# A hand-fixed instruction order written anew for a gated linear-attention and erf-feed-forward kernel

## The chip, the cores and the metric

The kernel runs on one core of a Trainium2 chip. The metric is device time in microseconds of one execution; lower is better. Three timed executions of the kernel before took 673.87, 674.10 and 674.49 us, a median of 674.1 us.

## What is computed

The reference takes `q`, `k`, `v` and complex gates `a_re`, `a_im` of shape (4 batches, 8 heads, 768 steps, 48 channels), and float64 weights `w_in` (384 x 2048) and `w_out` (2048 x 384). Cut to what matters:

```python
mag = np.sqrt(a_re * a_re + a_im * a_im)
scale = np.minimum(mag, 0.999) / (mag + 1e-06)
a_re_n, a_im_n = (a_re * scale, a_im * scale)
for t in range(S):                       # complex state of 48 x 48 per head
    S_re, S_im = ar * S_re - ai * S_im + kv[t], ar * S_im + ai * S_re
    y[t] = q[t] @ S_re
x = y.transpose(0, 2, 1, 3).reshape(3072, 384)
h = x @ w_in
sp = np.maximum(h, 0.0) + np.log1p(np.exp(-np.abs(h)))   # softplus
out = (h * erf(sp)) @ w_out
```

## The kernel before

The 3072 tokens are cut into 12 units of 256 tokens, three to a batch, and each unit into two chunks of 128 (`C = 2`). The order writes them as `u.c`, so `7.1` is the second chunk of unit 7.

**Gates.** `g` loads the gates, `m` squares them, `t` and `o` form the ratio of the two parts, `l` takes logarithms of the magnitude, `r` the arctangent. `a` turns the angles into running sums over time by a matmul with an upper triangle (`sum`, lines 914 and 915 or 995 and 997) and `F`, the rounded-off turn (line 1002); `s` takes sine and cosine (`CS`). `p` does the same for the decay: a running sum (line 1018, or 914 and 915) and its exponentials with both signs (`pr`). From unit 2 on a running sum is split into a high and a low fp32r part; the low part is made on VectorE (lines 961 and 987).

**Attention of one chunk.** `k`, `q` and `v` load; `K` and `Q` multiply by `pr` and `CS` (lines 1042 and 1047) and, from unit 2 on, transpose blocks on VectorE into `X`, which `M` moves by twelve small DMAs into `KQ` (line 1064). In units 0 and 1, `kT` and `qT` do this on TensorE. `A` forms the masked scores of four heads (matmuls at line 1084, mask on VectorE at line 1088). `S` carries the state (lines 1103, 1109, 1112). `Y` forms the result (line 1139), which ScalarE copies to `xT` (line 1141).

**Feed-forward of one unit.** It goes in two slabs of 1024 hidden channels, written `u.slab.i`. `h` is a tile of 256 channels: six matmuls into `hps` (line 1152) and a copy by ScalarE (line 1155). `x` is four ScalarE passes over a slab for the softplus and its inverse (exponential and logarithm). `e` is one quarter of a slab: a Gelu on ScalarE, then four VectorE operations (lines 1180 to 1186). `O` are the output products. Units 0 to 2 do them plainly (line 1220); from unit 3 on seven products of half the size (Strassen's way, line 1244) replace eight, with sums of `h` in `f` (lines 1197 and 1199) and of the products on VectorE (line 1252). The results are written to HBM from SP's queue (line 1211).

**Weights and checks.** `n` loads a piece of the float64 weights and narrows it on VectorE; `i` loads it again and looks for weights out of range (line 859); `b` forms sums of weights. `Z` checks at the end that all ranges seen allow this path: it reduces what was seen (lines 1310 to 1313), sums it over partitions with one matmul (line 1316), and compares (lines 1320 and 1321). Every engine then reads the flag `ok` and branches (lines 1388 and 1389); the slower path behind the branch is not taken here. `u4_2` and the like are four warm-up matmuls whose output nobody reads (line 1302).

**What sets the order.** Each of these steps is a Python generator, and each `yield` in it ends one part, most often the work of one engine. A string `ORDER` of 2303 names says which step goes on by one part next, and the instructions are issued in that order on every engine:

```python
with tc.manual_schedule():
    for nm in ORDER.split():
        if nm[0] == "u":
            steps[nm] = warm(int(nm[1:].split("_")[0]))
        next(steps[nm])
```

So the string fixes the list of each engine and of SP's DMA queue, and the order in which tiles take their turns in buffers. `ps_h` has two PSUM buffers for `hps`: a new `h` tile waits for the copy of the one before the last. The string was written outside the kernel by a planner that gives each part a place from assumed durations of operations, waits and transfers.

ScalarE's functions live in three sets of tables: logarithm and exponential, arctangent and sine, and Gelu. `act` issues a table load (line 786) when a function is not in the set that was loaded last, so the order of ScalarE's work decides how many loads there are:

```python
sets = [nm for nm, fs in TABLES.items() if func in fs]
if sets and T.get("table") != sets[0]:
    T["table"] = sets[0]
    scalar.preload_act_table_set(sets[0])
```

Of the kernel before, what the change touches and what calls it, by code (L numbers as in the profile page):

```python
# [49 lines left out]
u4_38 u4_21 u4_20 g0.0 g0.0 u2_39 g0.1 g0.1 t0.0 u2_34 u2_25 u4_2 m0.0 m0.0 m0.0 t0.0 t0.0 l0.0 l0.0 l0.0 l0.0  # L50
u2_40 o0.0 l0.0 m0.1 m0.1 m0.1 u2_23 p0.0 n0 n0 k0.0 t0.1 t0.1 t0.1 n0 n0 o0.1 n1 n1 l0.1 p0.0 l0.1 p0.0 l0.1
l0.1 r0.0 a0.0 l0.1 K0.0 r0.1 a0.1 q0.0 u2_24 Q0.0 u8_0 u8_1 a0.0 a0.0 u2_22 a0.0 s0.0 s0.0 s0.0 u2_41 a0.1 p0.1
p0.1 a0.1 n1 n1 g1.0 t1.0 g1.0 n3 p0.0 g1.1 Q0.0 qT0.0.1 qT0.0.0 qT0.0.0 K0.0 kT0.0.0 n3 a0.1 kT0.0.1 t1.0 p0.1
qT0.0.1 kT0.0.0 A0.0.0 t1.0 n3 o1.0 kT0.0.1 n3 v0.0 S0.0 r1.0 s0.1 a1.0 s0.1 a1.0 g1.1 A0.0.0 k0.1 p0.0 p0.1
q0.1 K0.1 Q0.1 S0.0 s0.1 K0.1 m1.1 m1.1 m1.0 a1.0 m1.0 Q0.1 m1.0 l1.0 l1.0 v0.1 A0.0.1 A0.0.1 n2 a1.0 n2 q1.0
t1.1 kT0.1.1 S0.1 l1.0 kT0.1.1 S0.1 l1.0 n2 l1.0 qT0.1.1 qT0.1.1 Y0.0 m1.1 n2 t1.1 t1.1 p0.1 S0.1 qT0.1.0
qT0.1.0 kT0.1.0 kT0.1.0 l1.1 Y0.0 l1.1 p1.0 p1.0 p1.0 l1.1 A0.1.0 A0.1.0 A0.1.1 A0.1.1 o1.1 r1.1 s1.0 l1.1 a1.1
s1.0 s1.0 n4 n4 Q1.0 k1.0 n4 l1.1 n4 Y0.1 Y0.1 a1.1 n5 n5 Q1.0 n5 K1.0 n5 p1.1 p1.1 g2.1 g2.0 t2 g2.1 g2.0 n6
v1.0 m2 m2 m2 v1.1 q1.1 t2 n6 K1.0 n7 h0.0.6 h0.0.6 v2.0 t2 l2 p1.1 l2 a1.1 l2 l2 p1.0 p1.1 a1.1 n6 Q1.1 n6 o2
n7 n7 l2 qT1.0.0 qT1.0.0 s1.1 n8 k1.1 l2 l2 a2.0 q2.0 h0.0.4 h0.0.4 s1.1 s1.1 qT1.0.1 h0.0.0 qT1.0.1 n7 Q1.1 n8  # L60
kT1.0.1 kT1.0.1 h0.0.2 r2 kT1.0.0 kT1.0.0 h0.0.2 h0.0.0 x0.0 a2.0 a2.0 S1.0 K1.1 S1.0 A1.0.1 p2.0 p2.0 p2.0
A1.0.0 h0.1.6 h0.1.6 a2.0 a2.0 a2.0 n8 A1.0.1 n9 x0.0 e0.0.2 p1.0 a2.0 n8 a2.1 A1.0.0 K1.1 a2.1 n9 a2.1 e0.0.0
S1.0 h0.1.0 h0.1.0 Y1.0 Y1.0 qT1.1.0 qT1.1.0 qT1.1.1 a2.1 n9 Q2.0 n9 qT1.1.1 a2.1 a2.1 a2.1 kT1.1.1 kT1.1.1 n10
n10 n10 p1.1 kT1.1.0 kT1.1.0 s2 s2 s2 p2.1 p2.1 p2.1 A1.1.1 A1.1.1 n10 k2.0 K2.0 A1.1.0 A1.1.0 S1.1 Q2.0 K2.0
S1.1 q2.1 K2.0 Q2.0 g3.0 g3.1 t3 t3 m3 g3.1 g3.0 t3 Q2.1 o3 m3 r3 h0.1.4 h0.1.4 Y1.1 Y1.1 h0.1.2 S2.0 a3.0
h0.1.2 m3 l3 l3 l3 h1.0.0 p2.0 n11 n11 Q2.1 n11 a3.0 S1.1 n11 S2.0 h1.1.0 x0.0 a3.0 a3.0 k2.1 K2.1 l3 l3 l3 l3
a3.0 M2.0 M2.0 M2.0 M2.0 A2.0.0 A2.0.1 K2.1 A2.0.1 A2.0.0 p2.0 p3.1 h1.0.0 x0.0 p3.0 a3.1 a3.1 e0.0.2 h1.0.2
h1.1.0 a3.1 p3.1 p3.1 a3.1 a3.1 e0.0.0 e0.0.2 e0.0.0 p3.0 p3.0 h1.0.2 e0.0.2 a3.1 e0.0.2 e0.0.0 a3.1 e0.0.0
e0.0.6 h1.0.4 h1.0.4 s3 K2.1 n12 k3.0 g4.0 e0.0.4 g4.0 g4.1 p3.0 q3.0 g4.1 Y2.0 n13 s3 s3 Q2.1 e0.0.4 e0.0.6
S2.0 e0.0.4 e0.0.4 e0.0.4 m4 m4 m4 l4 l4 t4 t4 l4 e0.0.6 e0.0.6 e0.0.6 h1.0.6 h1.1.6 M2.1 M2.1 M2.1 M2.1 l4 K3.0  # L70
n12 n12 l4 Q3.0 Q3.0 l4 K3.0 l4 Q3.0 h1.0.6 q3.1 p3.1 O0.0 v3.0 p3.0 O0.1 O0.3 O0.5 O0.7 A2.1.1 t4 A2.1.0 O0.2
A2.1.1 o4 O0.4 O0.6 h1.1.4 A2.1.0 k3.1 x0.1 x0.1 n12 x0.1 x0.1 K3.0 e0.1.2 e0.1.2 e0.1.2 e0.1.2 e0.1.0 e0.1.0
e0.1.2 h1.1.4 h1.1.6 Y2.0 r4 e0.1.0 e0.1.0 e0.1.0 v3.1 a4.0 a4.0 v2.1 Y2.1 e0.1.6 Y2.1 e0.1.6 e0.1.4 e0.1.6
e0.1.4 e0.1.4 e0.1.4 a4.0 a4.0 n13 e0.1.6 n13 h1.1.2 S3.0 S3.0 n13 h1.1.2 x1.0 x1.0 O0.9 h2.0.0 a4.0 a4.0 a4.0
e0.1.6 n15 e0.1.4 n15 n15 x1.0 M3.0 x1.0 h2.0.6 M3.0 M3.0 M3.0 A3.0.0 v4.1 n14 e1.0.0 K3.1 n15 a4.1 Q3.1 a4.1
e1.0.0 h2.0.0 e1.0.0 e1.0.0 e1.0.2 e1.0.2 n14 a4.1 a4.1 e1.0.2 p4.1 O0.8 e1.0.0 e1.0.2 e1.0.2 p4.1 p4.1 A3.0.1
h2.0.6 p4.0 O0.10 O0.11 p4.0 p4.0 h2.0.2 h2.0.2 g5.1 k4.0 n14 n14 k4.1 e1.0.4 e1.0.6 e1.0.6 g5.0 m5 t5 a4.1 g5.0
g5.1 e1.0.6 m5 K3.1 e1.0.4 e1.0.4 m5 e1.0.4 e1.0.4 A3.0.0 K3.1 p3.1 q4.1 Q3.1 A3.0.1 e1.0.6 e1.0.6 Q3.1 M3.1
M3.1 h2.1.0 h2.1.2 O0.12 h2.1.0 x1.1 t5 O0.14 a4.1 l5 O0.14 x1.1 l5 a4.1 h2.0.4 O0.13 S3.1 O0.15 O1.1 O1.3 O1.5
h2.1.2 O1.7 l5 l5 l5 S3.1 l5 K4.0 l5 x1.1 O0.15 x1.1 s4 S3.1 t5 o5 e1.1.2 e1.1.2 e1.1.2 e1.1.0 e1.1.0 e1.1.0  # L80
e1.1.2 e1.1.2 e1.1.0 e1.1.0 O1.0 h2.1.6 O1.2 O1.4 Y3.0 s4 r5 s4 K4.0 e1.1.4 e1.1.4 e1.1.4 e1.1.6 e1.1.6 e1.1.6
a5.0 q4.0 M3.1 p4.0 M3.1 A3.1.1 O1.6 A3.1.0 a5.0 A3.1.1 A3.1.0 e1.1.6 Q4.0 e1.1.4 K4.0 Q4.0 Q4.0 Q4.1 Q4.1 K4.1
h2.0.4 h2.1.6 h2.1.4 Y3.0 x2.0 Y3.1 v4.0 S4.0 a5.0 x2.0 a5.0 Y3.1 e1.1.4 S4.0 e1.1.6 p4.1 p4.1 M4.0 M4.0 x2.0
x2.0 M4.0 M4.0 O0.14 h3.0.0 e2.0.0 e2.0.0 e2.0.0 e2.0.2 e2.0.0 e2.0.2 e2.0.2 e2.0.2 e2.0.0 e2.0.2 p5.0 O1.9 p5.1
p5.0 p5.0 h3.0.0 h2.1.4 O1.11 O1.8 O1.10 e2.0.6 e2.0.4 a5.0 a5.0 e2.0.6 e2.0.4 a5.0 e2.0.4 e2.0.6 a5.1 a5.1 p5.1
# [24 lines left out]
h5.1.6 l8 O4.4 O4.4 O4.5 O4.5 O4.5 O4.5 e5.0.6 e5.0.4 h5.1.0 h5.1.0 O4.7 O4.7 O4.7 e5.0.4 e5.0.4 s7 s7 e5.0.6  # L110
# [1310 lines left out]
```

## Time and profile before

| what | value |
|---|---|
| median of the runs shown | 674.1 us |
| the profiled execution's own time | 674.05 us |
| its span, first to last instruction | 672.3 us |
| TensorE matmul rows, weight-load rows | 646.0 us (96%), 562.2 us (84%) |
| VectorE | 609.6 us (91%) |
| ScalarE | 578.7 us (86%), of it 120.6 us in 94 table loads |
| granted TensorE clock, mean | 0.998 |

The profile is of one execution; the sums of the prediction are made against its span. A row of the groups or of a timeline names the line, the engine, the operation, and output and inputs by the program's names; a bracket or the part after the last bar tells how long the engine was idle before and what ended that. A row of the waits reads: engine, what and line that waited, what it waited for, microseconds in total, times, and the longest. In the table by stages each engine has its busy microseconds and, in brackets, its number of instructions. A fp32 matmul appears as two passes in the rows, with a weight load for each. PE is TensorE, PEld its weight loads, DVE VectorE, ACT ScalarE, SP the engine that issues DMAs.

### The profile page before, as it was taken

The numbers are of one execution on the slowest core, as the hardware profiler recorded it, in microseconds if no ns is written. First come the engines' busy times: TensorE is split into PE (matmuls) and PEld (weight loads), VectorE is DVE, ScalarE is ACT, GpSimd is POOL, SyncE is SP. The second block draws the span as 40 slices with busy tenths as digits, with TensorE's granted clock in tenths as the row PEclk, the third lists the DMA queues.
The fourth block names the chain that finished last, engine by engine and source line by source line (L and its number), as shares of the span: only waits on it lengthen the run. The fifth ranks groups of instructions, "written<-read, shape, count | busy, mean of one in ns | idle before, by whom it ended". The sixth has DMA issues, their size and how long they took to land.

```text
span 672.3 us, 12307 instructions
## 1 busy us (share of the span) xinstructions
PE 646.0 (96%) x4728; PEld 562.2 (84%) x4728; DVE 609.6 (91%) x992; ACT 578.7 (86%) x762; POOL 1.1 (0%) x8
## 2 busy tenths in 40 slices
PE   8799999999999999999999999999999999999995
PEld 8678886876777768899898898999998899988885
DVE  5999999999989999999999999999999997868782
ACT  7999999999999999988997997998995895678800
POOL 0000000000000000000000000000000000000000
PEclk9999999999999999999999999999999999999999
DMA  9695767552256237227537736716726327211000
GB/s 252 159 247 153 169 138 143 118 129 48 36 114 123 43 61 187 54 44 169 93 51 165 130 60 149 134 26 158 137 44 168 57 34 207 39 34 47 1 24 29
DMA packets 282796, 70.23 MB, mean 104 GB/s; under 512 B 269396, under 2 KB 272488, under 8 KB 282728
## 3 DMA queue, kind: packets, MB, share of 16 engines
q1 hardware_dynamic: 280648, 68.96, 48.2%
q8 instruction: 39, 0.64, 0.4%
q10 hardware_dynamic: 2080, 0.39, 0.3%
q14 instruction: 29, 0.24, 0.1%
HBM read 48.82 MB, written 4.75 MB: 80 GB/s over the span
## 4 chain that ended last, share of the span: by engine, by line
ACT 41%; PE 24%; DVE 23%; issue 4%; DMA 4%; SPq 2%; POOL 0%; DVEq 0%; ACTq 0%; POOLq 0%
PE hps L1152 10%; ACT L786 10%; ACT z L787 7%; ACT yy L787 6%; ACT e L787 3%; DVE yy L1182 3%; DVE z L1180 3%; PE Y L1244 3%; DVE e L1184 2%; ACT h L1155 2%; ACT CS L787 2%; DVE h L1186 2%; PE X L1244 2%; ACT y L787 2%; ACT pr L787 2%
## 5 line engine op out<-in xcount | busy, mean ns | idle before, releaser
L1152 PE MATMUL hps<-xT,w_in_sb 128*128 128x256 f32 x1152 | 263.3, 381 | 1.8 <-ACT h L1155 1.2
L1152 PEld LDWEIGHTS hps<-xT,w_in_sb 128*128 128x128 f32 x1152 | 215.2, 190 | 34.7 <-ACT h L1155 5.1
L786 ACT ACT_TABLE_LOAD x94 | 120.6, 1283 | 3.7 <-issue 2.1
L1180 DVE TENSOR_TENSOR z<-z,yy 128x512 f32<-128x512 f32 x96 | 65.1, 686 | 17.7 <-ACT e L787 17.3
L787 ACT ACTIVATE e<-z 128x512 f32<-128x512 f32 x96 | 57.8, 627 | 24.7 <-DVE h L1186 23.9
L1155 ACT COPY h<-hps 128x512 f32<-128x512 f32 x96 | 54.2, 578 | 17.0 <-PE hps L1152 17.0
L1182 DVE SCALAR_TENSOR_TENSOR yy<-z,yy 128x512 f32<-128x512 f32 x96 | 65.1, 689 | 1.9
L1220 PE MATMUL ops<-w_out_sb,h 128*128 128x384 f32 x192 | 66.1, 487 | 0.0
L1186 DVE SCALAR_TENSOR_TENSOR h<-e,h 128x512 f32<-128x512 f32 x96 | 64.5, 686 | 1.4
L1184 DVE TENSOR_TENSOR e<-e,yy 128x512 f32<-128x512 f32 x96 | 64.6, 686 | 1.1
L1084 PEld LDWEIGHTS sc<-KQ 96*128 96x128 f32 x384 | 47.0, 191 | 8.2 <-issue 5.2
L1220 PEld LDWEIGHTS ops<-w_out_sb,h 128*128 128x128 f32 x192 | 35.6, 190 | 20.2 <-DVE h L1186 0.6
L1084 PE MATMUL sc<-KQ 96*128 96x128 f32 x384 | 49.9, 278 | 2.4 <-DMA KQ<-X 1.1
L787 ACT ACTIVATE z<-h 128x2048 f32<-128x2048 f32 x24 | 45.8, 1910 | 4.9 <-DVE seen L859 3.2
L787 ACT ACTIVATE yy<-z 128x2048 f32<-128x2048 f32 x24 | 45.8, 1909 | 0.7 <-DVE seen L859 0.2
L787 ACT ACTIVATE yy<-yy 128x2048 f32<-128x2048 f32 x24 | 45.9, 1911 | 0.6
L787 ACT ACTIVATE z<-z 128x2048 f32<-128x2048 f32 x24 | 45.8, 1909 | 0.4
L1139 PE MATMUL y<-A,v 128*32 128x128 f32 x768 | 34.1, 276 | 2.0 <-DVE A L1088 1.5
L1088 DVE TENSOR_TENSOR A<-sc,triu 128x512 f32<-128x512 f32 x48 | 32.0, 677 | 1.1 <-PE sc L1084 1.1
L1103 PEld LDWEIGHTS kv<-v,kt 128*96 128x96 f32 x320 | 29.8, 165 | 1.8 <-issue 0.7
L1103 PE MATMUL kv<-v,kt 128*96 128x48 f32 x320 | 29.8, 246 | 0.0
L1139 PEld LDWEIGHTS y<-A,v 128*32 128x32 f32 x768 | 21.1, 109 | 9.4 <-DVE A L1088 2.6
(114 smaller groups left out, 1070.5 us busy)
## 6 DMA issues: line engine op xcount, KB each, us to landing
KQ<-X SPq DMA_DIRECT2D x240, 64.0 KB
raw<-in_moe_w_in_dram SPq DMA_DIRECT2D x8, 768.0 KB
raw<-in_moe_w_out_dram SPq DMA_DIRECT2D x8, 768.0 KB
again<-in_moe_w_in_dram SPq DMA_DIRECT2D x8, 768.0 KB
ar<-in_a_re_dram SPq DMA_DIRECT2D x24, 192.0 KB
k<-in_k_dram SPq DMA_DIRECT2D x24, 192.0 KB
q<-in_q_dram SPq DMA_DIRECT2D x24, 192.0 KB
v<-in_v_dram SPq DMA_DIRECT2D x48, 96.0 KB
```

What stands on the lines that cost most here:

```text
L786: scalar.preload_act_table_set(sets[0])
L787: scalar.activation(func=func, **kw)
L1084: nc.tensor.matmul(out=ps[:, j, :], lhsT=head("k", g * HG + j, u, c), rhs=head("q", g * HG + j, u, c), start=True, stop=True)
L1103: nc.tensor.matmul(out=kv[0:D2, j, :], lhsT=T["kt", u, c][:, j].rearrange("p u d -> p (u d)"), rhs=side(T["v", u][:, c, j // 2], j % 2), s ...
L1139: nc.tensor.matmul(out=ps[b * QUAD:(b + 1) * QUAD, i, :], lhsT=lhsT, rhs=rhs, start=start, stop=stop)
L1152: nc.tensor.matmul(out=ps[:, e, :], lhsT=w_in_sb[:, (sl * SLAB + i) // 2, kd, e * P:(e + 1) * P], rhs=T["xT", u][:, kd, :], start=(kd == 0 ...
L1155: scalar.copy(out=T["h", u, sl][:, i:i + 2, :], in_=ps)
L1180: vector.tensor_tensor(out=z, in0=z, in1=y, op=OP.mult)
L1182: vector.scalar_tensor_tensor(out=y, in0=z, scalar=-2.0, in1=y, op0=OP.add, op1=OP.mult)
L1184: vector.tensor_tensor(out=e, in0=e, in1=y, op=OP.mult)
L1186: vector.scalar_tensor_tensor(out=h, in0=e, scalar=1.0 / RT2, in1=h, op0=OP.add, op1=OP.mult)
L1220: nc.tensor.matmul(out=ps, lhsT=lhsT, rhs=w_out_sb[:, i, :], start=i == HALF, stop=i == KF - 1)
```

## The change

Only the string `ORDER` is replaced. It holds the same 2303 names, each as often as before: no instruction is added or taken away by the string itself, but ScalarE's table loads follow from its order. The planner was run anew with somewhat longer operations, waits and transfers than the medians it had used, and was allowed to place the split running sums beside the result matmuls. Nearly every place moves. The beginning and the end of the diff:

```diff
@@ -47,125 +47,125 @@
 ORDER = """
-u4_38 u4_21 u4_20 g0.0 g0.0 u2_39 g0.1 g0.1 t0.0 u2_34 u2_25 u4_2 m0.0 m0.0 m0.0 t0.0 t0.0 l0.0 l0.0 l0.0 l0.0
-u2_40 o0.0 l0.0 m0.1 m0.1 m0.1 u2_23 p0.0 n0 n0 k0.0 t0.1 t0.1 t0.1 n0 n0 o0.1 n1 n1 l0.1 p0.0 l0.1 p0.0 l0.1
-l0.1 r0.0 a0.0 l0.1 K0.0 r0.1 a0.1 q0.0 u2_24 Q0.0 u8_0 u8_1 a0.0 a0.0 u2_22 a0.0 s0.0 s0.0 s0.0 u2_41 a0.1 p0.1
-p0.1 a0.1 n1 n1 g1.0 t1.0 g1.0 n3 p0.0 g1.1 Q0.0 qT0.0.1 qT0.0.0 qT0.0.0 K0.0 kT0.0.0 n3 a0.1 kT0.0.1 t1.0 p0.1
...
-e10.1.2 f10.1 f10.1 h11.0.2 x11.0 x11.0 x11.0 x11.0 e11.0.4 e11.0.4 e11.0.4 h11.1.6 e11.0.0 e11.0.0 e11.0.4
-e11.0.0 e11.0.4 e11.0.0 e11.0.0 h11.1.2 h11.1.2 e11.0.2 e11.0.2 e11.0.6 e11.0.2 e11.0.6 e11.0.6 e11.0.2 e11.0.2
-e11.0.6 O10.1 h11.1.0 O10.1 h11.1.0 h11.1.4 h11.1.4 x11.1 x11.1 x11.1 x11.1 e11.1.2 O10.2 O10.2 e11.0.6 O10.0
-O10.3 O10.4 O10.6 O10.5 e11.1.0 O10.5 O10.7 O10.5 O10.5 O10.7 O10.7 O10.8 O10.9 O10.4 O10.10 e11.1.2 e11.1.0
-e11.1.2 e11.1.0 e11.1.2 e11.1.0 O10.11 e11.1.2 e11.1.0 f11.0 O10.11 O10.11 O10.12 O10.13 e11.1.4 e11.1.4 e11.1.6
-e11.1.6 e11.1.4 O10.13 e11.1.6 e11.1.4 e11.1.6 e11.1.4 e11.1.6 f11.1 f11.1 O11.0 O10.13 O11.1 O11.3 O11.1 O11.2
-O11.2 f11.0 O11.4 O11.5 O11.5 O11.4 O11.6 O11.5 O11.5 O11.7 O11.7 O11.12 O11.7 O11.8 O11.9 O11.10 O11.11 O11.13
-O11.11 O11.11 Z Z O11.13 O11.13 Z
+u4_2 u4_38 u4_21 u8_0 u2_39 u4_20 g0.0 g0.0 g0.1 g0.1 u2_34 u2_41 t0.0 t0.0 m0.0 m0.0 m0.0 m0.1 l0.0 l0.0 m0.1
+l0.0 t0.1 u2_22 t0.0 o0.0 m0.1 l0.1 t0.1 l0.1 l0.1 l0.0 l0.0 p0.0 p0.0 p0.0 u8_1 n0 u2_40 r0.0 a0.0 k0.0 t0.1 n1
+l0.1 n0 l0.1 o0.1 n0 a0.0 q0.0 n0 u2_24 n1 n1 a0.0 r0.1 a0.0 Q0.0 s0.0 K0.0 g1.0 n1 u2_23 p0.1 a0.1 a0.1 u2_25
+n3 n3 v0.0 q0.1 s0.0 s0.0 Q0.0 qT0.0.0 K0.0 kT0.0.1 kT0.0.0 p0.0 p0.1 t1.0 Q0.1 n3 m1.0 p0.1 a0.1 t1.0 qT0.0.0
...
+O9.11 i15 O9.13 h11.1.6 e10.1.4 e10.1.2 e10.1.2 f10.1 f10.0 O9.11 O9.13 f10.0 f10.1 O9.13 O9.11 h11.0.2 x11.0
+x11.0 x11.0 x11.0 e11.0.4 e11.0.4 e11.0.4 O10.0 h11.1.6 e11.0.0 e11.0.0 e11.0.4 e11.0.0 e11.0.4 e11.0.0 e11.0.0
+h11.1.2 h11.1.2 e11.0.2 e11.0.2 e11.0.6 e11.0.2 e11.0.6 e11.0.6 e11.0.6 e11.0.6 i15 e11.0.2 e11.0.2 i15 h11.1.4
+h11.1.4 h11.1.0 h11.1.0 x11.1 x11.1 x11.1 x11.1 e11.1.2 O10.1 O10.3 O10.2 e11.1.0 O10.6 O10.1 O10.4 O10.2 O10.5
+O10.4 O10.5 O10.5 O10.5 O10.7 O10.7 Z O10.7 O10.8 O10.9 e11.1.2 e11.1.0 e11.1.2 e11.1.0 e11.1.2 e11.1.0 O10.10
+O10.11 e11.1.2 e11.1.0 e11.1.4 f11.0 e11.1.4 O10.12 O10.13 O10.11 e11.1.6 O10.11 O10.13 e11.1.6 e11.1.4 e11.1.6
+e11.1.4 e11.1.6 e11.1.4 O10.13 e11.1.6 f11.1 f11.1 O11.0 O11.3 O11.1 Z O11.2 O11.1 f11.0 O11.2 Z O11.4 O11.5
+O11.5 O11.5 O11.5 O11.6 O11.7 O11.7 O11.7 O11.4 O11.8 O11.9 O11.10 O11.11 O11.11 O11.11 O11.12 O11.13 O11.13
+O11.13
 """
```

Between the second slab of unit 3 and the first of unit 4 (from `x3.1` to `x4.0`) both orders do the exponentials of unit 6's decay (`p6`). The order before has `p6.0 p6.0 p6.0 O2.15 e3.1.6 e3.1.6 e3.1.4 ... p6.1 p6.1 p6.1`, with the Gelu of two quarters between the chunks; the new one has `e3.1.6 p6.1 p6.0 p6.1 ... p6.1 p6.0 p6.1 p6.1 ... p6.0 p6.0 p6.0`, with no Gelu between the exponentials.

## The prediction

> **What bounds the kernel now.** I read the busy table by stages first: three engines are above 86% over the whole span, so the page's averages settle nothing.
>
> ```profile
> core 0: us, PE busy (x) PEld busy (x) DVE busy (x) ACT busy (x) POOL busy (x), PEclk, DMA share, GB/s
> 0.00:20.00 20.00, 17.41 (x106) 15.47 (x106) 12.18 (x32) 14.97 (x30) 1.08 (x8) 1.00 0.98 236
> ...
> 100.00:200.00 100.00, 98.16 (x584) 73.42 (x583) 94.33 (x143) 98.73 (x123) 0.00 (x0) 1.00 0.50 97
> 200.00:300.00 100.00, 98.01 (x698) 79.50 (x698) 96.27 (x155) 98.11 (x122) 0.00 (x0) 1.00 0.44 86
> ...
> 400.00:500.00 100.00, 99.36 (x766) 92.22 (x765) 96.42 (x155) 90.29 (x116) 0.00 (x0) 1.00 0.54 110
> 500.00:600.00 100.00, 98.95 (x785) 90.99 (x784) 86.70 (x138) 75.37 (x90) 0.00 (x0) 1.00 0.43 93
> ```
>
> TensorE's own row says 98% everywhere; its weight loads (PEld) tell more: 73 and 80 us per 100 up to 300 us while ScalarE is at 98 to 99, then 91 to 92 while ScalarE falls to 90 and 75. So ScalarE (and close behind it VectorE) paces the first 300 us and TensorE the rest. A microsecond of ScalarE counts before 300 us and hardly after.
>
> Next, how much TensorE loses. I charge each instruction the median time from its start to the next start on its engine where nothing was waited for (an hps matmul of two passes 0.432 us, a 192-column output product 0.325 us, and so on). TensorE's whole list comes to 629.6 us, VectorE's to 591.7, ScalarE's to 559.7. What the clock is ahead of such a sum is that engine's lag. TensorE's lag is 11.2 us at 40 us, 15.0 at 100, 22.5 at 300, 30.8 at 620, and 35.1 at 660; after its last product (664.75 us) 7.5 us of closing remain. 629.6 + 35.1 + 7.5 = 672.2, the span. Nothing in the change touches the 629.6, so all it can do lies in those 42.6 us.
>
> Third, the wait views: what the lag is made of late on, and what waits are there to be won.
>
> ```profile
> ACT e L787 <- DVE h L1186: 23.9, 15, 3.9
> DVE z L1180 <- ACT e L787: 17.3, 16, 5.6
> ACT h L1155 <- PE hps L1152: 17.0, 13, 2.8
> DVE out L1252 <- PE Z L1244: 7.0, 2, 5.6
> ```
>
> The large ones are ScalarE and VectorE waiting, mostly after 300 us, where they have time to spare: 17.0 of the 23.9 and 12.8 of the 17.0 fall between 300 and 600. On TensorE's own row the waits between 300 and 600 sum to only 3.3 us.
>
> **The change part by part.** No instruction changes but ScalarE's table loads; 2303 places are permuted.
>
> *Start (0 to 20 us).* Before:
>
> ```profile
> 11.20 0.49 ACT L787 ACTIVATE pr<-sum 128x384 f32<-128x384 f32 x1 [1.05 <-PE sum L1018]
> ...
> 13.01 1.28 ACT L786 ACT_TABLE_LOAD   x1
> ...
> 16.39 0.58 ACT L787 ACTIVATE F<-sum,column 128x384 f32<-128x384 f32 x1
> ```
>
> Now 32 warm-up matmuls instead of 26 stand ahead of the first running sum. Six more at 0.224 us put that sum 1.3 us later (12.5 instead of 11.2 us); ScalarE has two more activations to do first (2 x 0.54), so its wait there is about 1.3 instead of 1.05 and the first table load slips about 0.6 us. Then F follows its own producer directly (before, two activations stood between): 1.0 us of wait for the running sum. The wait behind F (0.62 before the cosine) shrinks to about 0.1. Together ScalarE reaches its second table load about 1.0 us later. Queued behind it are unit 0's cosine and sine, then keys, queries and scores. SP's list keeps its first seven transfers; the imaginary gates of unit 1 go from its eighth place to its fourteenth, behind a row of decays that is ready near 13 us, and are read near 24 by the same count, so they have some 7 us (an estimate from these starts). I take +1.0 on ScalarE; bounds 0 (the sum earlier than I reckon) and +2.
>
> Here a rule speaks against the change. The granted clock is 1.00 in 0 to 20 us. The Trainium skill (TensorE: Matmul & The Clock Gate, Part 1) says TensorE falls to half clock after an idle window of about 3.4 us. By the row the regrouped warm-ups cost nothing: the longest idle stretch in the first 40 us is below 2 us, and with 1 us more it stays below the rule's window. By the rule, were it closed for one window, 3.4 us of TensorE work would take 6.8, an estimate of +3.4 us; I keep that for the range.
>
> *ScalarE's tables.* The list has 92 loads instead of 94. Up to slab 8 (unit 3, second half) both have 40 ahead of the first exponential; at the next slab 42 instead of 44. The two saved lie where the trace stands between 247 and 267 us: both decay sums now share one visit to the exp set. Further on the difference comes and goes, and stays two.
>
> ```profile
> L786 ACT ACT_TABLE_LOAD x94 | 120.6, 1283 | 3.7 <-issue 2.1
> ```
>
> By this row it is 2 x 1.283 = 2.6 us. The Trainium skill (ScalarE: Activation LUTs, What ACT_TABLE_LOAD costs) adds a drain of 1.38 us per switch, 5.3 us for the two. The trace shows no drain: 3.7 us idle before all 94 loads, and the activation after one starts 1.29 us after it (13.01 to 14.31). The row decides: 2.6.
>
> *ScalarE-paced stretch.* What a later ScalarE costs TensorE is read from place sums: work ahead of a copy on ScalarE plus its start (2.1) plus TensorE's work behind the matmul that waits for that copy. Before: copy of an h tile with 248.5 us ahead, 240.4 of TensorE done: 2.1 + 248.5 + 389.2 = 639.8. This stays at 639 to 640 until 263 us of TensorE's list. With ScalarE's lag there (14.9, less the 2.1) the last such place gives 639.5 + 12.8 = 652.3; the trace has TensorE's 629.6 + lag 22.2 = 651.8, so the reading holds. After: the largest sum is 640.4, but early (ScalarE 84.5, TensorE 75.8); the last high one is 639.0 at ScalarE 212. Beyond TensorE's 240 it is 636.1, and 631.2 beyond 280 (633.9 before). With the lag at 212 (11.3) and the late start, 639.0 + 9.2 + 1.0 = 649.2. So ScalarE would let TensorE go 2.5 us sooner, the start included. But VectorE then sets it: its sums at 240 to 290 are 628.1 and 628.0 before and 627.7 and 626.7 after; with its lag of 25.6 less 2.0 that is 651.7 before and about 650.3 to 651.3 after. VectorE's lag itself holds 4.7 us of waiting for the Gelu between 60 and 300 us, of which an earlier ScalarE takes some. I take **-1.5**. Bounds: -3 (most of those waits go) and +2.5: between 60 and 300 us TensorE's places stand closer to their producers in the new order. With the old lags, 56 of 94 such places have under 1 us in hand, against 44 of 99.
>
> *TensorE-paced stretch (300 to 620).* In the new order TensorE's places stand on average 5 us behind their producers instead of 2.5. Of the 3.3 us of waits I take **-1.0**; bounds -3.3 and +1. ScalarE will wait more (for hps and for VectorE), which is covered as long as TensorE has work. The KQ transfers' issue moves with their X; their waits in TensorE's row are 1.1 us in all.
>
> *End.* The last h tiles, the last Z and the products stand as before, within one or two products. But the validity check moves:
>
> ```profile
> 663.29 1.46 PE L1244 MATMUL W<-w_out_sb,h 128*128 128x192 f32 x8
> 664.76 0.09 PEld L1316 LDWEIGHTS all<-sums,column 128*1 128x1 f32 x2 [0.30 <-DVE sums L1313]
> 664.79 0.36 DVE L1252 SCALAR_TENSOR_TENSOR out<-W,out 128x192 f32<-128x192 f32 x1
> 665.57 0.15 DVE L1321 TENSOR_REDUCE ok<-within 1x1 int32<-1x6 f32 x1
> ```
>
> Before, every engine reads the flag after 665.72, behind the check; then 6.6 us of reading it, branching and closing. After, the check's matmul stands 14.5 us ahead of TensorE's end and the flag is long there; what the closing follows is the last product (664.75) or the last output write (665.15). That is 0.57 to 0.97 us: **-0.8**. Its VectorE work (1.1 us) moves into the last slab's chain, ahead of one difference of halves that has over 1 us in hand; were that cover gone, +0.5.
>
> Sum: 672.3 - 1.5 - 1.0 - 0.8 = 669.0 span. The profiled execution took 674.05 with a span of 672.3, 1.75 around it, and is the median of the runs shown (674.1): **670.8**.
>
> **Rivals.** (a) *No change* (672.8 to 675.4): VectorE's list keeps TensorE where it is at 290 us, and only the end is won. For it: VectorE's sum falls by only 0.4 at one place. 674.1 - 0.8 + 0.2 = 673.5. (b) *TensorE starves early*, the other side: between 60 and 300 us its matmuls come before their data. For it: the places short of time sum to 21 us instead of 8.5 under the old lags. If half of the additional 12.5 became lag, +6.2, and nothing were regained after 300, 674.1 + 6.2 - 0.8 = 679.5. It decides once early starving passes 3.3 + 1.3 us; against it: an early delay repeats at the next place only if it is larger there. (c) *The early slack is worth more*: VectorE's 4.7 and TensorE's 3.3 go wholly, 674.1 - 4.7 - 3.3 - 0.8 = 665.3; against it: VectorE would then have no wait left anywhere.
>
> **How the numbers follow.** Runs of this kernel lie within 0.1% of each other, so 0.2% (1.35 us) is about what can be told from no change. Forecast 0.43, (a) 0.14, (b) 0.32, (c) 0.11. Faster: forecast and (c), 0.54; same 0.14; slower 0.32. The range leaves out the far half of (c) and of (b)'s upper part: 666.0 to 680.0; the forecast's own, from its bounds, 667.5 to 672.7.
>
> **What would show it.** Start: second table load near 20.2 us (19.19 before), and a wait of F for the sum near 16 us. Tables: 92 loads. Middle: TensorE's weight loads in 200 to 300 us above 79.5; in 60 to 300 the Gelu wait of VectorE below 4.7. Late: TensorE's waits in 300 to 600 below 3.3. End: closing after the last product below 7.5. Wrong, if weight loads in 100 to 300 us fall, or waits for h copies and A tiles grow on TensorE's row; then (b).

## The result, and the profile after

The changed kernel takes 668.98 us (median of six runs, 668.56 to 669.80) beside 673.69 for the kernel before: a ratio of 0.9931, 95% interval [0.9918, 0.9943]. It is 4.7 us faster where 3.3 were forecast. The profiled execution took 668.56 us with a span of 666.7; before, 674.05 and 672.3. So the two traces differ by 5.6 us of span, and it is this difference that the stages below add up to. Part of it, about 0.9 us, is not the order's but chance at the start, as shown below.

The table by stages of the changed kernel; the columns are those explained with the profile before, and PEclk (the granted clock) is the number behind POOL's.

```profile
core 0: us, PE busy (x) PEld busy (x) DVE busy (x) ACT busy (x) POOL busy (x), PEclk, DMA share, GB/s
0.00:20.00 20.00, 16.42 (x106) 14.37 (x106) 12.77 (x33) 14.97 (x30) 1.09 (x8) 1.00 0.97 236
100.00:200.00 100.00, 95.79 (x572) 73.03 (x570) 90.54 (x139) 94.79 (x117) 0.00 (x0) 0.97 0.44 84
200.00:300.00 100.00, 99.73 (x705) 81.64 (x704) 95.58 (x156) 96.13 (x121) 0.00 (x0) 1.00 0.46 90
...
400.00:500.00 100.00, 99.48 (x772) 92.60 (x771) 96.40 (x156) 91.90 (x118) 0.00 (x0) 1.00 0.55 112
500.00:600.00 100.00, 100.00 (x792) 92.69 (x792) 89.08 (x142) 77.21 (x94) 0.00 (x0) 1.00 0.42 92
```

From 200 us on TensorE's weight loads fill more of each stage than before (81.64 for 79.50, 92.69 for 90.99). Between 100 and 200 us every engine has lost something (TensorE 98.16 to 95.79, VectorE 94.33 to 90.54, ScalarE 98.73 to 94.79), and the clock stands at 0.97 where it was 1.00. All three engines lose 2 to 4 us in the same stretch: that hints at one event rather than at a rate.

The waits of the whole span:

```profile
ACT e L787 <- DVE h L1186: 23.7, 15, 3.9
DVE z L1180 <- ACT e L787: 23.6, 22, 4.2
ACT h L1155 <- PE hps L1152: 14.9, 12, 2.9
...
PE sum L914 <- ACT pr L787: 4.4, 2, 3.9
```

VectorE's wait for the Gelu has grown from 17.3 to 23.6. The last row is the one to read: one TensorE wait of 3.9 us; before, TensorE's longest between 60 and 300 us was 1.0.

TensorE's lag, reckoned as in the prediction (the clock, less the median work of TensorE's list up to there), says when it happens. "Moved up" is the first experiment below.

| at, us | 40 | 100 | 140 | 160 | 200 | 300 | 400 | 600 | 660 |
|---|---|---|---|---|---|---|---|---|---|
| before | 11.3 | 15.3 | 16.8 | 17.8 | 18.9 | 22.9 | 26.6 | 30.8 | 35.1 |
| after | 11.1 | 15.8 | 15.8 | 23.0 | 23.3 | 24.5 | 25.9 | 27.4 | 31.6 |
| moved up | 11.1 | 15.8 | 17.0 | 16.9 | 17.3 | 18.5 | 19.9 | 21.5 | 30.7 |

(The last column of the third row is past that kernel's last products.) From one column to the next, the new order changes the lag by -1.0 up to 140 us, +6.2 between 140 and 160, -3.6 up to 300, -5.0 up to 600 and -0.1 to the last products. The closing behind the last product is 2.2 us shorter. Together -5.7, the 5.6 of the spans.

**The first -1.0 is mostly not the order's.** In every trace the warm-up passes start at 0.21 us intervals and fall to 0.11 at one moment, the moment at which the trace's record of the granted clock begins; the 1.00 that the table shows for the first 20 us says nothing of the time ahead of it. That moment lies at 7.7 us in the trace of before, at 4.9 in that of the changed kernel, and between 4.4 and 7.7 in the fourteen traces of this study. Count TensorE's passes, before (two rows) and after (two rows), and in the changed order with only the end altered (the kernel with the check last, below), where the moment lies at 7.6:

```profile
4.00:6.00 2.00, 2.00 (x12) 2.00 (x11) 0.37 (x1) 1.85 (x5) 0.00 (x0) 1.00 1.27 252
6.00:8.00 2.00, 2.00 (x12) 2.00 (x12) 1.32 (x4) 1.73 (x5) 0.00 (x0) 1.00 1.06 354
...
4.00:6.00 2.00, 2.00 (x16) 2.00 (x15) 0.00 (x0) 1.86 (x5) 0.00 (x0) 1.00 1.26 257
6.00:8.00 2.00, 2.00 (x20) 2.00 (x19) 1.78 (x5) 1.66 (x5) 0.00 (x0) 1.00 1.08 348
...
6.00:8.00 2.00, 2.00 (x13) 2.00 (x13) 1.72 (x5) 1.76 (x5) 0.00 (x0) 1.00 1.08 351
```

In that last kernel every TensorE instruction comes 0.9 us later than in the changed kernel, from 30 us up to the wait at 140. In the old order a moment 3.3 us earlier (the kernel with the check early) brings every instruction 1.3 us forward, still so at 500 us. So a trace can carry up to 1.3 us of its start to its end. With before's start the changed kernel would stand about 0.9 us later than it does here (an estimate from these two traces of one order), and the spans would differ by some 4.7, as the medians do. What sets the moment the runs don't show.

The +6.2 is one event. The timeline of the changed kernel, rows of VectorE, ScalarE and TensorE in order of their start:

```profile
136.62 5.34 PE L1152 MATMUL hps<-xT,w_in_sb 128*128 128x256 f32 x24
137.14 0.96 DVE L849 SCALAR_TENSOR_TENSOR w_out_sb<-raw,word 128x768 uint32<-128x768 uint32 x1
138.18 0.58 ACT L1155 COPY h<-hps 128x512 f32<-128x512 f32 x1 [4.19 <-issue]
141.96 1.15 ACT L787 ACTIVATE e<-z 128x512 f32<-128x512 f32 x2
142.62 0.69 DVE L1180 TENSOR_TENSOR z<-z,yy 128x512 f32<-128x512 f32 x1 [4.07 <-ACT e L787]
145.85 0.69 PE L914 MATMUL sum<-parts,triu_r 128*128 128x384 f32 x1 [3.89 <-ACT pr L787]
147.18 7.66 PE L1152 MATMUL hps<-xT,w_in_sb 128*128 128x256 f32 x24 [0.32 <-ACT h L1155]
```

ScalarE stands idle for 4.19 us ahead of its copy of an `hps` tile at 138.18 us, "until issue": the timeline names no releaser. What the copy writes tells more. Unit 2's `h` takes its buffer from the pool of the raw weights (line 1147, tag `raw`), and the last reader of raw weights in that buffer is VectorE's operation at line 849, begun 137.14. The records of ScalarE's own sequencer agree: it waits at the copy's line until 138.14, for VectorE's semaphore and for that of the DMA of the narrow piece `n15`. VectorE had taken `n15` late, though its DMA had landed at 103.9. Behind the waiting copy stood an exponential and the Gelus; VectorE waited for a Gelu (4.07), TensorE for a sum's buffer (3.89). And when TensorE went on, the same 24 passes of `hps` took 7.66 us instead of 5.34.

The remaining lines that answer to those shown of before. The start on ScalarE, the table loads' group, and the end:

```profile
11.64 0.87 ACT L787 ACTIVATE pr<-sum 128x384 f32<-128x384 f32 x2
...
15.98 0.58 ACT L787 ACTIVATE F<-sum,column 128x384 f32<-128x384 f32 x1 [1.00 <-PE sum L995]
...
19.05 1.28 ACT L786 ACT_TABLE_LOAD   x1
```

```profile
L786 ACT ACT_TABLE_LOAD x92 | 118.0, 1283 | 3.5 <-issue 2.1
```

```profile
645.64 0.20 PE L1316 MATMUL all<-sums,column 128*1 128x6 f32 x2
...
658.63 2.76 PE L1244 MATMUL W<-w_out_sb,h 128*128 128x192 f32 x16
...
661.43 0.36 DVE L1252 SCALAR_TENSOR_TENSOR out<-W,out 128x192 f32<-128x192 f32 x1 [2.04 <-PE W L1244]
```

The second table load is at 19.05 (19.19 before), not at 20.2; with before's start it is at 19.95 (see the last part). There are 92 loads. The validity check's matmul is 13 us ahead of the last product. From the last product (661.4) to the end of the span (666.7) it is 5.3 us, 7.5 before.

### The profile page after: what moved, and what is told of

It reads as the page before. It is cut to its first block, busy times and chain, and to the rows that moved or that the text cites. A ratio compares the mean times of both kernels' runs of the same rounds, so it can differ in the third digit from the quotient of the medians.

```text
span 666.7 us, 12316 instructions
## 1 busy us (share of the span) xinstructions
PE 643.9 (97%) x4728; PEld 563.0 (84%) x4728; DVE 606.6 (91%) x992; ACT 574.5 (86%) x760; POOL 1.1 (0%) x8
## 4 chain that ended last, share of the span: by engine, by line
PE 51%; ACT 30%; DVE 10%; issue 3%; DMA 3%; SPq 1%; ACTq 0%; DVEq 0%
PE hps L1152 20%; PE ops L1220 7%; ACT L786 6%; ACT z L787 5%; ACT yy L787 4%; PE X L1244 4%; PE Y L1244 4%; PE y L1139 4%; PE sc L1084 4%; PE Z L1244 3%; ACT y L787 2%; ACT th L787 2%; PE kv L1103 2%; DVE yy L1182 2%; DVE z L1180 2%
## 5 line engine op out<-in xcount | busy, mean ns | idle before, releaser
L1152 PEld LDWEIGHTS hps<-xT,w_in_sb 128*128 128x128 f32 x1152 | 217.4, 191 | 34.1 <-ACT h L1155 2.8
L1180 DVE TENSOR_TENSOR z<-z,yy 128x512 f32<-128x512 f32 x96 | 64.6, 686 | 24.2 <-ACT e L787 23.6
```

The lines of the kernel that those rows point to most:

```text
L1152: nc.tensor.matmul(out=ps[:, e, :], lhsT=w_in_sb[:, (sl * SLAB + i) // 2, kd, e * P:(e + 1) * P], rhs=T["xT", u][:, kd, :], start=(kd == 0 ...
L1180: vector.tensor_tensor(out=z, in0=z, in1=y, op=OP.mult)
```

## The experiments

Every kernel was timed 4 to 11 times, in one of three groups, each with the kernel before beside it (medians 674.06, 673.43 and 673.97 us). Changes of `ORDER` are shown cut to the names that move.

### The stall at 138 us: taken away in two ways

The first experiment moves the three VectorE parts of `n15` up behind those of `n13`:

```diff
-e0.1.6 n13 e0.1.4 a4.0 e0.1.6 S3.0 K3.1 K3.1 n15 Q3.1 n15 n15 a4.1 a4.1 n14 h2.0.6 x1.0 h2.0.6
+e0.1.6 n13 n15 n15 n15 e0.1.4 a4.0 e0.1.6 S3.0 K3.1 K3.1 Q3.1 a4.1 a4.1 n14 h2.0.6 x1.0 h2.0.6
```

> The changed kernel, with the three VectorE parts of the sixteenth narrow weight tile (word, word, w_out_sb of n15) moved up behind those of n13, so that the raw buffer that unit 2's first h tile takes is free some 20 us earlier, and the copy of hps at 138 us needs no wait (4.2 us in the changed kernel). Theory A, the stall is carried to the end: 4 us less than the changed kernel's 669.0, near 665, and the granted clock of the stretch from 100 to 200 us back from 0.97 to 1.00. Theory B, VectorE carries only its own share (its lag stood 1.7 to 2 us higher behind the stall): near 667.2. Theory C, ScalarE and VectorE pace the stretch to 300 us anyway and have made it up by then: 668.5 to 669.5, with TensorE's lag at 160 us back from 23 to 18, but near 24 at 300 as it was.

Measured: 663.09 us (662.52 to 664.20), ratio to before 0.9843 [0.9830, 0.9856]. That is 5.9 us below the changed kernel, more than theory A's 4. VectorE's last operation on `n15` starts at 132.90 instead of 137.14, only 4 us earlier and not 20, but early enough. The stretch from 100 to 200 us and the `hps` passes of this kernel:

```profile
100.00:200.00 100.00, 99.44 (x598) 75.22 (x592) 95.28 (x146) 99.38 (x122) 0.00 (x0) 1.00 0.48 93
```

```profile
137.79 5.34 PE L1152 MATMUL hps<-xT,w_in_sb 128*128 128x256 f32 x24
...
143.32 5.42 PE L1152 MATMUL hps<-xT,w_in_sb 128*128 128x256 f32 x24
```

The copy no longer waits, the clock is back at 1.00, and the lag at 160 us is 16.9 instead of 23.0. That 6.1 is still 5.9 at 600 us (21.5 against 27.4): nothing behind the stall makes it up. Theories B and C fall. This kernel is also the fastest of the study, 1.6% below before.

The second leaves VectorE alone and moves the waiting copy on ScalarE behind the exponential and the first Gelu:

```diff
-n14 h2.0.6 x1.0 h2.0.6 x1.0 e1.0.0 e1.0.0 A3.0.1
+n14 h2.0.6 x1.0 x1.0 e1.0.0 e1.0.0 h2.0.6 A3.0.1
```

> The changed kernel, with the waiting copy of hps (unit 2, second of slab 0) moved on ScalarE behind the exponential of yy and the first Gelu that stood behind it; VectorE's order stays. If what hurts is the work queued behind the waiting copy (theory A), its wait falls from 4.2 us to about 0.5, VectorE's wait at z (4.1 us, for that Gelu) and TensorE's (3.9 us, for the decays' sum) go too, and the time is near 665, as with the weight tile moved. Theory B: 667. Theory C: 668.5 to 669.5. If the copy itself were what TensorE waits for, nothing would be gained: 669 or more.

Measured: 663.77 us, 0.9851 [0.9837, 0.9865]. Its timeline:

```profile
138.07 0.59 ACT L1155 COPY h<-hps 128x512 f32<-128x512 f32 x1 [0.21 <-issue]
...
143.26 5.79 PE L1152 MATMUL hps<-xT,w_in_sb 128*128 128x256 f32 x24 [0.71 <-ACT h L1155]
```

The copy runs at the same moment as in the changed kernel (138.07 against 138.18), so a late copy as such costs nothing. The price was the work queued behind it on ScalarE's in-order list: place an exponential, a Gelu and the table load between them ahead of the wait, and 5.2 of the 5.9 us are gone.

### What the stall costs beyond its wait: the clock

The wait on TensorE was 3.9 us, the loss 5.9. The changed kernel in stretches of 2 us, same columns as above:

```profile
142.00:144.00 2.00, 0.00 (x0) 0.00 (x0) 1.34 (x3) 1.98 (x4) 0.00 (x0) 1.00 0.00 0
144.00:146.00 2.00, 0.15 (x1) 0.15 (x1) 2.00 (x5) 1.99 (x5) 0.00 (x0) 0.72 0.00 0
146.00:148.00 2.00, 1.68 (x4) 1.08 (x5) 1.93 (x4) 1.98 (x5) 0.00 (x0) 0.50 0.02 3
148.00:150.00 2.00, 2.00 (x6) 1.55 (x6) 2.00 (x4) 1.99 (x4) 0.00 (x0) 0.50 1.07 212
150.00:152.00 2.00, 2.00 (x7) 1.61 (x6) 1.97 (x3) 1.97 (x3) 0.00 (x0) 0.58 0.89 175
```

The granted clock falls to one half about 3 us into the idle stretch and stays there for 6.8 us (each stretch's share of the drop from 1.00 to 0.50, times 2 us: 1.12 + 2 + 2 + 1.68). The wait's length alone doesn't set this time. In the same order with the check last, in its profiled execution, a wait as long is followed by 3.4 us at one half (stretches of 2 us from 146 at 0.90, 0.50 and 0.75), and the passes behind it take 6.86 instead of 7.66:

```profile
146.79 0.44 PE L914 MATMUL sum<-parts,triu_r 128*128 128x384 f32 x1 [3.96 <-ACT pr L787]
...
148.12 6.86 PE L1152 MATMUL hps<-xT,w_in_sb 128*128 128x256 f32 x24 [0.71 <-ACT h L1155]
```

Two experiments put work into the hole. The first took a free-looking PSUM tile for 16 unread matmuls:

```diff
+                steps[nm] = warm(int(nm[1:].split("_")[0]), *((ps_a, "a") if nm.endswith("a") else ()))
...
-h2.0.0 h2.0.0 t5 a4.1 m5
+h2.0.0 h2.0.0 t5 u16_99a a4.1 m5
```

> The changed kernel with its stall, and 16 matmuls of a unit matrix (0.22 us each, 3.6 us) added on TensorE into a PSUM tile that nobody reads, ahead of the sum that waited 3.9 us at 142 us. The stall stays; only TensorE's idleness goes. If the granted clock behind the stall is what it costs beyond the wait (the 24 matmuls of hps took 7.66 us at 147 us, 5.34 elsewhere): 2.3 us less than the changed kernel's 669.0, near 666.7, and these 24 at 5.3 us. If the clock follows something else: 669 or, with the added work, up to 670.

Measured: 681.94 us, 1.0118 [1.0103, 1.0134], a miss that doesn't answer the question, since TensorE stood idle longer:

```profile
155.34 6.33 PE L1302 MATMUL unread<-ident 128*128 128x128 f32 x32 [12.65 <-DVE A L1088]
```

The unread tile took its turn in the scores' two buffers, so its first matmul waited for VectorE's mask (line 1088), which stood behind VectorE's own wait in the same stall. A filler brings its own dependence.

The second fills the hole with work whose buffer was free already: the first half of unit 2's third `h` tile is multiplied three times more and overwritten.

```diff
-        for e in range(2):
+        for e in ((0,) * 3 + (0, 1) if (u, sl, i) == (2, 0, 0) else range(2)):
```

> The changed kernel with its stall, and TensorE kept busy in it in another way: ahead of unit 2's third h tile its first half is multiplied three times more (9 fp32 matmuls of two passes, 0.445 us each, 4.0 us; they are overwritten, the sums stay as they are). The wait of 3.9 us ahead of the next sum is filled with them, and the tile's copy is not due before 146.5 us. If the granted clock costs 2.3 us behind the idle stretch: 666.7, and the next 24 passes of hps at 5.3 us instead of 7.66. If not: 669.0.

Measured: 667.64 us (667.28 to 667.74), 0.9902 [0.9888, 0.9917]. Its rows, with 18 more passes in the first:

```profile
137.41 9.23 PE L1152 MATMUL hps<-xT,w_in_sb 128*128 128x256 f32 x42
...
147.85 5.79 PE L1152 MATMUL hps<-xT,w_in_sb 128*128 128x256 f32 x24 [0.71 <-ACT h L1155]
```

The clock stays at 1.00 through this stretch, and the passes take 5.79 instead of 7.66, although TensorE now does 4 us more work. By medians 1.3 us are won, by the ratios to before 2.0, where 2.3 were expected. In the trace these passes end at 153.64 instead of 154.84, 1.2 sooner, although this trace stood 0.8 us later already ahead of the change (137.41 against 136.62; its faster pace begins at 6.4 us instead of 4.9). That makes 2.0 as well, and with the wait's 3.9 it is the loss of 5.9; 0.4 of the expected gain goes into a longer wait for a copy of `h`. That the long passes were the clock's doing is shown; the size is 1.3 to 2.0.

### The validity check at the end

Its three parts moved in the old order, and nothing else (the other kernel does the reverse in the new order):

```diff
 O10.5 O10.7 O10.7
+Z
 O10.8 ... O11.1 O11.3 O11.1
+Z
 O11.2 O11.2 f11.0
+Z
 O11.4 ... O11.11 O11.11
-Z Z
 O11.13 O11.13
-Z
```

> The kernel before, with only the validity check's three parts moved ahead as in the changed kernel (in the last output stretch of unit 10 and 11). The forecast's term for the end: 0.57 to 0.97 us less than before, 672.8 to 673.1. The rival, read off the closing stretches of the two profiles (7.5 us from the last product to the end before, 5.3 after): TensorE's slow branch runs beneath the last products, 2.2 us less, near 671.5.

> The changed kernel, with the check's three parts put back to the very end, as before. The forecast's term: 0.8 us more than the changed kernel, 669.8. The rival: 2.2 us more, 671.2, and closing after the last product back at 7.5 us.

Measured: 671.23 us (0.9964 [0.9952, 0.9977]) with the check early in the old order, 2.8 below the 674.06 beside it by medians, 2.4 by the ratio; 671.88 us (0.9971 [0.9961, 0.9982]) with it last in the new order, 2.9 above the changed kernel. Both fit the rival's 2.2 and not the forecast's 0.8. In the traces the closing goes from 7.5 to 5.4 us in the old order, and from 5.3 back to 7.3 in the new. The end of the old order with the check early:

```profile
662.40 1.46 PE L1244 MATMUL W<-w_out_sb,h 128*128 128x192 f32 x8
...
663.90 0.36 DVE L1252 SCALAR_TENSOR_TENSOR out<-W,out 128x192 f32<-128x192 f32 x1 [0.74 <-PE W L1244]
```

From there to the end of its span (669.3) it is 5.4 us. The sequencers' own records, which the timeline leaves out, say more. Before, all five engines read the flag at 665.75, 1.0 us after the last product. TensorE's branch then took 4.24 us (666.67 to 670.91); its next record ends last, at 671.01, but SyncE's ends only 0.1 earlier. In the changed kernel GpSimd and ScalarE are through by 653.1. TensorE reads the flag at 658.32 and its branch takes 3.50 us (658.92 to 662.42), beneath its own last matmuls. Only VectorE and SyncE are left: VectorE reads the flag at 661.44, 0.05 us after the last product, and goes on at 665.19 (its branch starts at 662.05); SyncE ends at 665.39. So 0.9 us come from the earlier start, and 1.3 because reading and branching take 3.95 us from VectorE's read on, instead of 5.26. Whether that is TensorE's branch being out of the way or fewer engines branching at once, the runs don't tell apart.

### Table loads

A first attempt to drop two loads from the old order moved one decay sum with its exponentials to the next one's:

```diff
-p5.0 O1.9 p5.1 p5.0 p5.0 h3.0.0 ... a5.1 a5.1 p5.1 p5.1
+O1.9 p5.1 h3.0.0 ... a5.1 a5.1 p5.0 p5.0 p5.0 p5.1 p5.1
```

> The kernel before, with one edit: unit 5's first decay sum and its two exponentials move behind a pair of Gelus, next to those of the second sum (at 188 us, where ScalarE has no idle time for 45 us). 92 table loads instead of 94. If ScalarE sets TensorE's pace there, 2.6 us less: 671.5. If VectorE sets it (the forecast's reading at 240 to 290 us), 0 to 1 less: 673.1 to 674.1.

Measured: 679.34 us, 1.0085 [1.0071, 1.0099]: both theories missed, on the other side.

```profile
192.24 0.69 PE L914 MATMUL sum<-hi,triu_r 128*128 128x384 f32 x1 [4.36 <-DVE F L1002]
```

The loads are two fewer, but the moved sum takes its PSUM buffer behind another one, whose reader `F` on VectorE is still far off. TensorE stands for 4.4 us, the clock falls to 0.50 there as well (6.8 us), and the whole costs 5.9 us, net of what the two loads may have brought. It is a stall like the changed kernel's, made by hand; what two saved loads are worth stays unmeasured.

So loads were priced by adding some, where nothing else moves: a redundant load (of the set already there) ahead of three Gelus, once where ScalarE has no idle time and once late.

```diff
     def erf_times_h(u, sl, i):
-
+        T["table"] = None if (u, sl) == (2, 1) else T["table"]
```

> The kernel before, with three redundant table loads added on ScalarE and nothing else moved: one more ahead of each of the last three Gelus of unit 2's second slab (205 to 211 us, where ScalarE has no idle time). 3 x 1.283 = 3.85 us of ScalarE work. If ScalarE sets TensorE's pace up to 260 us, the time grows by 3 to 4 us: 677 to 678. If VectorE sets it, as the forecast took it at 240 to 290 us, by 0 to 1: 673.5 to 674.7. [...]

Measured: 678.27 us, 1.0061 [1.0048, 1.0074], 4.1 us [3.2, 5.0] for 3.85 us of loads. ScalarE's added time counts in full at 205 us, and there is no room for the drain that the prediction weighed, which would make it 8. Whether ScalarE time that is saved counts as fully between 240 and 290 us, where the forecast saw VectorE behind it, this does not test.

```diff
-        T["table"] = None if (u, sl) == (2, 1) else T["table"]
+        T["table"] = None if (u, sl) == (9, 0) else T["table"]
```

> The kernel before, with three redundant table loads on ScalarE in unit 9's first slab (528 to 536 us, where TensorE's list sets the pace and ScalarE is busy 75 of 100 us). The forecast's reading, that a microsecond of ScalarE hardly counts there: 0 to 0.5 us more, 673.5 to 674.2. If the chain of unit 9's h tiles to TensorE's output products is short of time: up to 3.85 more.

Measured: 676.31 us, 1.0039 [1.0024, 1.0054], 2.6 us [1.6, 3.6]. The second theory in part: in a stretch where ScalarE is busy for 75 of 100 us, about two thirds of its added time still reach the end. Between 540 and 560 us TensorE's lag grows by 3.1 where it grew by 0.5 before, and new waits stand on its rows:

```profile
PE y L1139 <- DVE A L1088: 1.1, 1, 1.1
...
PE Z L1244 <- DVE out L1252: 0.7, 1, 0.7
```

### Which half of the order wins what

Three kernels join the two orders at the first exponential of a unit's first slab. The first half is kept as it is in one kernel, and the names left over follow in the other's order.

> The order of before up to the first exponential of unit 4's first slab (268 us), then the order of the changed kernel for all that is left (the check's early place with it). In the two profiles TensorE's lag grows from 300 us to 600 by 7.9 us before and by 2.9 after, and the weight loads' waits there sum to 11.8 and 7.4 us. Theory: the late gain belongs to the late order itself and does not need the middle: 5 us from it and 2.6 from the check, 674.1 - 7.6 = 666.5. Rival: the slack of the late stretch is built up by the middle's order: only the check's part, near 671.5.

Measured: 666.96 us, 0.9904 [0.9888, 0.9920]. The theory holds: behind the seam the lag goes from 21.3 at 300 us to 25.8 at 600, 4.5 us; it is 2.9 in the changed kernel and 7.9 before. The late order brings most of its gain along, whatever stood ahead of it.

> The order of the changed kernel with the sixteenth weight tile moved up (the run at 663.1), up to the first exponential of unit 4's first slab, then the order of before (the check at the end). TensorE's lag at 260 us was 18.5 there and 21.8 before. Theory: the early half's gain is carried: 674.1 - 3.3 = 670.8, and with the other half's 7.6 it makes up the 11 us between that run and before. Rival: the late order of before is paced by its producers and gives it back: 673 or more.

Measured: 673.80 us, 1.0005 [0.9996, 1.0014]. The rival holds: TensorE's lead of 3.5 us at 260 us is gone at 280 (lag 22.3; before 22.1).

```profile
277.62 4.54 PE L1152 MATMUL hps<-xT,w_in_sb 128*128 128x256 f32 x12 [2.23 <-ACT h L1155]
```

TensorE waits for a copy that ScalarE starts at 277.00, behind a chain of exponentials, a table load, two Gelus and another load. Before's own trace has that copy at 280.27, with a TensorE wait of 0.29 us: the later TensorE was just in time there, the earlier one runs into ScalarE. Then 12 passes take 4.54 us instead of 2.75: the clock falls behind this wait of 2.2 us too, for 3.4 us (stretches of 2 us at 0.95, 0.50, 0.69).

> The order of the changed kernel with the sixteenth weight tile moved up, now as far as the first exponential of unit 6's first slab (364 us), then the order of before. At 360 us TensorE's lag is 19.6 in that kernel and 24.8 in before. Behind it, before's order adds 4.1 us more up to 600 us than the other does, and the check at the end 2.7. Theory: beyond 300 us TensorE's list sets the pace and the lead is kept, 663.1 + 4.1 + 2.7 = 669.9. Rival: as with the seam at 268 us, before's order waits for its producers and gives the lead back: 673 or more.

Measured: 672.15 us, 0.9968 [0.9955, 0.9981], between the two. At 360 us, ahead of the seam, the lead over before is 5.2 us in the trace with `n15` moved up, but 3.6 in this one, though both have the same order up to there (this one is 0.7 us later from its start on, and 1.7 by 350). At 400 us 1.8 are left, and at 600 us 1.5. Whether the old order's places give it back or the seam itself spoils it (ScalarE waits 1.7 us for VectorE's angles there) the run doesn't tell apart.

## Why the prediction was right, and where it was not

The forecast was -3.3 us; -4.7 came, the right sign and near the right size, but by luck: with the start evened out, the term up to 300 us promised about 4 us too much and the one behind it 4 too little, and they cancelled. What is left over is the end, whose gain was put 1.4 too small.

**Start, +1.0: it came, and the traces hide it.** The wait of `F` is there (1.00 at 15.98, as forecast). With the faster pace beginning at 7.6 us, as in before, the new order (check last) has:

```profile
12.53 0.87 ACT L787 ACTIVATE pr<-sum 128x384 f32<-128x384 f32 x2 [0.82 <-PE sum L1018]
...
19.95 1.28 ACT L786 ACT_TABLE_LOAD   x1
```

That is 12.5 instead of 11.2, as forecast, and a second load 0.8 us later than before; with the pace beginning at 4.4 us in both orders it is 1.0 (18.89 against 17.91). In the changed kernel's own trace the load stands at 19.05 because its warm-ups ran faster from 4.9 us on. What the prediction had wrong here is a reading: "the granted clock is 1.00 in 0 to 20 us". The half pace stood there, unseen in that row, and its length changed between the two traces.

**Tables, 2 x 1.283 = 2.6.** 92 loads, as said. The rule of the Trainium skill with a drain of 1.38 us per switch (ScalarE: Activation LUTs, What ACT_TABLE_LOAD costs) was set aside for the row, and three added loads at 4.1 us bear the row out (3.85 against 8.0), though they only load again the set that is there; for the real switches the row itself speaks, with 3.5 us of idle time ahead of all 92. The next step, "but VectorE then sets it", allowed TensorE a gain of 0.4 to 1.4 us; without the stall its lag at 300 us is 4.4 lower, so VectorE did not hold it there. How much of the 4.4 the two loads brought was not separated.

**ScalarE-paced stretch, -1.5 with bounds -3 and +2.5: a sum that hid two large terms.** Up to 300 us it was +1.6 in the traces (about +2.5 with before's start), inside the bounds but of the wrong sign: the stall's +6.2, and -4.6 for the rest. Without the stall the lag at 300 us is 18.5, 4.4 below before, which is beyond the forecast's best bound. The step that failed is the method: place sums bound a stretch by its engines' totals, and a wait between two engines over a shared buffer, VectorE's line 849 ahead of ScalarE's copy, was never among the pairs summed. It summed up many places; one pair below zero was enough. Of its signs here, the weight loads rose from 200 to 300 us as forecast, but VectorE's Gelu wait between 60 and 300 us went to 8.8 and not below 4.7 (4.0 without the stall).

**Clock, set aside as a range item.** The Trainium skill (TensorE: Matmul & The Clock Gate, Part 1) gives an observation window of about 3.4 us, and a half clock after an idle one. Here the row decides and agrees in kind: half clock lasted 3.4 us with an idle stretch of 2.2, 3.4 in one trace and 6.8 in another with 3.9, and 13.7 with 12.7, that is one, two and four windows. The prediction looked for it only at the start, where no idle stretch after the first warm-up was above 1.2 us; and its reading, that below the window's length nothing happens, did not hold for the 2.2 us. Its price, 3.4 us for one window, was reckoned too high as well: 12 passes of `hps` lost 1.8 us in a window that was full of work, and the changed kernel some 2 us in its two (5.9 less the wait of 3.9), in part of which TensorE stood idle.

**TensorE-paced stretch, -1.0 with bounds -3.3 and +1: -5.0.** The step that failed is "of the 3.3 us of waits". That was TensorE's matmul row. A weight load waits too, often for the same data, and TensorE's lag goes with its loads. Some of the waits between 300 and 600 us, before:

```profile
PEld hps L1152 <- ACT h L1155: 1.2, 3, 0.4
PEld Y L1244 <- DVE h L1199: 1.2, 1, 1.2
...
PEld W L1244 <- DVE out L1252: 0.8, 1, 0.8
```

and after:

```profile
PEld sum L914 <- ACT pr L787: 1.1, 2, 0.9
...
PEld W L1244 <- DVE out L1252: 0.3, 1, 0.3
...
PEld hps L1152 <- ACT h L1155: 0.2, 1, 0.2
```

All rows of PEld come to 11.8 us before and 7.4 after, -4.4, about half of it with no releaser named; those of PE to 3.3 and 0.9. The lag grows by 5.0 less. The other traces agree: against before, PEld's idle time in this stretch changes by -4.7 to +2.9 us and the growth of the lag by -5.1 to +3.1, and the two lie within 0.6 us of each other in twelve of thirteen kernels, where PE's rows miss by up to 2.6. (The thirteenth is the one with 16 unread matmuls, shifted by 13 us: 2.1.) The mechanism that the prediction named, TensorE's places standing 5 us instead of 2.5 behind their producers, fits: the old order loses two thirds of 3.85 us that ScalarE is made late (unit 9), so its slack was short of that. That the new order would lose less was not run and stays argued.

**End, -0.8: -2.2 in the trace, -2.4 to -2.9 alone.** The step "what the closing follows is the last product or the last output" counted only the start of the closing, and had that right (0.9). Its length was put at no change, but reading the flag and branching takes 1.3 us less when TensorE, ScalarE and GpSimd have done it beneath the last products.

**Rivals.** (b) had forecast +6.2 of early starving, and +6.2 was measured, but by coincidence: its sum was over many places that stand short of time, and what came was one wait for a buffer. Its "nothing regained after 300" did not hold, and so the sign went the other way. Its own signs did not show either: between 60 and 300 us TensorE's waits for copies of `h` went from 0.3 to 0.5 us, and those for `A` tiles from 1.5 to none shown. (a), only the end won, falls with the late 5 us. (c)'s total of 665.3 is nearest to the 663.1 measured without the stall, but not its sources: there VectorE's Gelu wait is still 4.0 of 4.7 us, TensorE's fell from 3.3 to 0.9, and the end brought more than 0.8.

## What to carry to other kernels

When an order is rewritten, compare each instruction's place with that of the last user of its buffer on every other engine, not only with its data's producer: one pair that comes out negative stops an in-order engine with all that is queued behind it. Here moving either of the two brought more than the whole rewriting had. Read what a better order can win for TensorE from the waits of its weight loads, not from its matmuls'. Let slow sequencer work, such as the branch at the end, start while TensorE still has matmuls queued. And before two single traces are subtracted, see whether their warm-ups ran at the same pace for as long.

## What the hardware showed that was not expected

- The granted clock fell to 0.50 during or just after TensorE waits of 2.2, 3.9, 4.0, 4.4 and 12.7 us, and not at waits of 1.5 us in the run with three more loads. It stayed there for 3.4, 6.8, 3.4, 6.8 and 13.7 us: multiples of 3.41 that the wait's length alone doesn't fix.
- The first warm-up passes ran at half pace until 4.4 to 7.7 us, differently in each trace, and in one and the same order the difference (up to 1.3 us) reached the end undiminished.
- An idle stretch filled with 4 us of useless matmuls made the kernel 1.3 us faster by medians, 2.0 by the ratios.
- TensorE's branch on the flag took 3.3 to 4.3 us in its records, and it can lie beneath matmuls that were issued before it.
